# A gated linear attention with a two-layer network: its first step written on its own, and the order of the next three steps

## The chip, the cores and the metric

The kernel runs on one core of a Trainium2 chip. The metric is device time in microseconds (us) of one execution. Engines are named as the profile names them: PE multiplies matrices (PEld is its weight load), DVE and ACT work element by element, POOL is a third such engine and also issues DMAs, SP only issues DMAs.

## What is computed

```python
f = 1.0 / (1.0 + np.exp(-f_logit))                # B=4, H=8, S=768, D=48
for t in range(S):
    state = f[:, :, t, :, None] * state + np.einsum('bhd,bhe->bhde', k[:, :, t], v[:, :, t])
    y[:, :, t] = np.einsum('bhd,bhde->bhe', q[:, :, t], state)
x = y.transpose(0, 2, 1, 3).reshape(3072, 384)
h = x @ w_in                                      # 384 -> 2048
out = (np.maximum(h, 0.0) + alpha * np.minimum(h, 0.0)) @ w_out
```

## The kernel before, in words

The sequence is cut into 6 chunks of 128 times and the 4 batches into 2 pairs. A **step** is one chunk of one pair, so there are 12 steps, numbered by time: steps 0 and 1 are the first chunk of the two pairs (c is 0), steps 2 and 3 the second, and so on. Each step runs four generators, and an order written by hand as strings (FIRST for steps 0 to 3, USUAL for the rest) says which one is advanced next, up to its next `yield`. PE, DVE and ACT execute strictly in that order. SP and POOL are left to the framework's scheduler.

The letters of the order are these; a digit repeats the letter.

- `P` advances prepare (L258) of this step and `Q` that of the next step. It has six parts: (1) loads of f, q, k, v, a sigmoid and the products of q with up to three decays (qd, L287); (2) prefix and suffix scans (L317, L319); (3) scaled keys k4 and the first terms of us; (4) and (5) the other terms, kh, ks and q3; (6) the copies of q3 into A (L419).
- `O` advances carry, in two parts: first the products off (L444, L454), their copies into ad and A (L458, L462), the transposed keys pk (L471) and their copies ksn (L474); then the state products pd (L484) and moved(0), which puts them into vs (L500 for c = 0).
- `S` advances attend (six parts): for each of the two batches the score products raw (L520) and qu (L535) with masked copies into ad (L526, L541, L557); two parts of copies of ad into A (L563); the output products py (L574); and last moved(1), the copies of py to y (L583) and the ten DMAs that lay y out as xT (L603). In step 0 alone xT comes from twelve PE instructions with a constant `dense` (L592) and three ACT copies.
- `n` advances network of the **previous** step: eight parts with a product ph (L618) of 24 or 12 PE instructions, an ACT copy neg (L623) and two DVE gates (L625) each, then the second product. Of step 0 (`plain`) this is four parts of po (L638), the last of which ends with two ACT copies o (L644) and the stores: 12 parts. For the others it is seven half-size products (L657) with sums on DVE (L702): 13 parts.
- `a` and `b` load a piece of w_in and w_out (eight each) and convert it on ACT (L224, L225); `w` and `v` finish a piece on DVE (L234). ph number f of step 0 needs piece f of w_in. `W` (five parts, the first without work) forms differences of w_out on DVE (L721), which the networks after step 0 read.

PSUM has eight banks: two two-bank tiles (`psa`) for the attention products and four one-bank tiles (`psn`) for the network. At the start 52 small matmuls (L736) run on PE before any input is there. The buffers of f, q, k are single, so the next step's loads wait for the readers of this one.

In the order before, five of the six parts of prepare of step 1 stand in step 0 (`Q`), five of step 2 in step 1, and five of step 3 in step 2.

Of the kernel before, what the change touches and what calls it, by code (L numbers as in the profile page):

```python
# [17 lines left out]
C = 128  # L18
# [8 lines left out]
IDLE = 52  # L27
# [11 lines left out]
def flat(first, usual, steps=12):  # L39
    out = []  # L40
    left = {}
    for n in range(steps + 1):
        for key in (first[n] if n < len(first) else usual).split():
            for _ in range(int(key[1:] or 1)):
                k = key[0]
                if k in "awbvW":
# [12 lines left out]
def kernel(  # L59
# [60 lines left out]
    psn = ctx.enter_context(tc.tile_pool(name="psn", bufs=4, space=bass.MemoryType.PSUM))  # L120

    def pair(name):
        return psa.tile([128, 2, 512], F32, tag="pair", name=name)

    def bank(name):
        return psn.tile([128, 512], F32, tag="net", name=name)
# [35 lines left out]
    nc.gpsimd.memset(mquad, 0.0)  # L162
    for m in range(1, NB):
        lo = UO[m] + (4 if m == 1 else 0)
        n = NB - m
        nc.gpsimd.tensor_copy(mquad[:, lo:lo + 4 * n].rearrange("p (i r) -> p i r", r=4),
                              inq[:, 0:n].unsqueeze(2).broadcast_to((128, n, 4)))
    mhalf = const.tile([128, VW], F32, tag="mhalf", name="mhalf")
    nc.gpsimd.memset(mhalf, 0.0)
    for half in range(2):  # L170
        for m in range(1, NQ):
            n = NQ - m
            lo = 16 * half + 4 if m == 1 else VO[m] + 4 * n * half
            nc.gpsimd.tensor_copy(mhalf[:, lo:lo + 4 * n].rearrange("p (i r) -> p i r", r=4),
                                  inq[:, NQ * half:NQ * half + n].unsqueeze(2).broadcast_to((128, n, 4)))
# [7 lines left out]
    make_identity(nc, ident)  # L183
    nc.gpsimd.tensor_scalar(om, om, -1.0, 1.0, ALU.mult, ALU.add)


    dense = work.tile([128, DM], F32, tag="o", name="dense")
    nc.gpsimd.memset(dense, 0.0)
    for par in range(2):
        nc.gpsimd.tensor_copy(dense[:, (2 + par) * D:(3 + par) * D], ident[:, 64 * par:64 * par + D])  # L190
# [66 lines left out]

    def prepare(bp, c, x):  # L258

        i = f"{bp}_{c}"  # L260
        b0 = U * bp
        loads = nc.gpsimd if bp or c else nc.sync

        def load(name, src, bufs=2):
            t = work.tile([128, W], F32, tag=name, name=f"{name}_{i}", bufs=bufs)
            loads.dma_start(out=t.rearrange("p (u x) -> p u x", u=U),
                              in_=src[b0:b0 + U, c].rearrange("u p h t -> p u (h t)"))
            return t

        f = quads(load("f", fT, 1))  # L270
        q = load("q", qT, 1)
        k = x["k"] = load("k", kT, 1)

        for cc in range(NC2):
            t_, _ = halves(cc)
            loads.dma_start(out=vs[bp][t_, cc, :, 0:DM], in_=v[b0:b0 + U, c, t_].rearrange("u t d -> t u d"))


# [40 lines left out]
        nc.vector.tensor_tensor_scan(ss[:, ::-1], fs[:, ::-1], ones[:, ::-1], 0.0, ALU.mult, ALU.add)  # L319
        yield  # L320
# [57 lines left out]
        ended(0)  # L378
        if c:
            earlier(3)  # L380
        else:
            near(2, 1)
        ended(1)
        if c:
            earlier(4)
        else:
            nc.vector.tensor_tensor(k16[:, :, 0:16].rearrange("p g (i r) -> p g i r", r=4),
                                    k4.rearrange("p (g i r) -> p g i r", i=NB, r=4)[:, :, 0:NQ],
                                    g16[:, :, 0:NQ].unsqueeze(3).broadcast_to((128, G, NQ, 4)), ALU.mult)
        started(1)  # L390
        if c:
            earlier(5)
        else:
            near(3)
        yield
        if c:
            earlier(6)
        nc.vector.tensor_tensor(ks[:, :, 0], kh, f32[:, 1:G:2].broadcast_to((128, GC, DB)), ALU.mult)
        if c:
# [3 lines left out]
        else:  # L403
            nc.vector.tensor_tensor(q16.rearrange("p g (i r) -> p g i r", r=4), q4[:, :, NQ:NB], g16[:, :, NQ:NB].unsqueeze(3).broadcast_to((128, G, NQ, 4)), ALU.mult)
# [27 lines left out]
    def carry(bp, c, x):  # L432

        i = f"{bp}_{c}"
        q3, ks, kh, f64 = (x[n] for n in ("q3", "ks", "kh", "f64"))
        off = pair(f"off_{i}")
        for u in range(U):
            for hp in range(HP):
                for cc in range(NC2):
                    g = (u * HP + hp) * NC2 + cc  # L440
                    o = (u * HP + hp) * DB
                    for par in range(2):
                        r_ = rows(par)
                        nc.tensor.matmul(off[CH * cc:CH * cc + DB, par, o:o + DB],  # L444
                                         lhsT=kh[r_, g], rhs=q3[r_, g, 2], start=True, stop=True)
        if not c:
            for u in range(U):
                for hp in range(HP):
                    for j in range(NJ):
                        g = (u * HP + hp) * NJ + j  # L450
                        o = U * HP * DB + (u * HP + hp) * 16
                        for par in range(2):
                            r_ = rows(par)
                            nc.tensor.matmul(off[DB * j:DB * (j + 1), par, o:o + 16], lhsT=x["k16"][r_, g],  # L454
                                             rhs=x["q16"][r_, g], start=True, stop=True)
            for u in range(U):
                o = U * HP * DB + u * HP * 16
                nc.scalar.copy(ad[:, u, :, :, 16:DB], off[:, :, o:o + HP * 16].rearrange("p r (h t) -> p r h t", h=HP))  # L458
        for cc in range(NC2):
            s_ = slice(CH * cc, CH * cc + DB)  # L460
            for par in range(2):
                nc.scalar.copy(A[s_, :, par * HP:(par + 1) * HP, CH * cc + DB:CH * (cc + 1)],  # L462
                               off[s_, par, 0:U * HP * DB].rearrange("p (u h t) -> p u h t", u=U, h=HP))


# [333 lines left out]
```

## Time and profile before

| what | value |
|---|---|
| runs, median (range) | 622.3 us (620.87 to 622.85), 3 runs |
| profiled execution | span 622.1 us; the page gives no other time for it, and it lies within the runs |
| busy share of the span | PE 95%, PEld 85%, DVE 80%, ACT 40%, POOL 10% |
| first ph of the network of step 0 | starts 48.98 us |
| first ph of the networks of steps 1, 2 and 3 | start 102.47, 152.34 and 199.98 us |
| each step from then on | 47.7 us |
| DMA busy share, 0 to 40 us | 0.83 to 1.05 |

Times are counted from the start of the span. In a timeline row the first number is the start, the second the time from the first start to the last end of a merged group; brackets hold the idle time of the engine before it and what ended it. In a windows row each engine has its busy time and the number of instructions. A matmul of the program in fp32 shows as two records, each with a weight load of its own.

### The profile page before, as it was taken

How to read it: one execution, taken by the hardware profiler on the slowest of the kernel's cores; microseconds unless marked ns; L12 is line 12 of the kernel's file. 1: busy time of each engine (PE TensorE's matmuls, PEld its weight loads, DVE VectorE, ACT ScalarE, POOL GpSimd, SP SyncE). 2: the span in 40 equal slices, each digit the busy share in tenths (PEclk: the TensorE clock that was granted, in tenths of full speed). 3: DMA queues.
4: the chain of work that ended last, by engine and by line, in shares of the span. 5: the costliest groups of instructions: out<-in, count | busy, mean ns of one | idle time of the engine just before them, and what ended most of it. 6: DMA issues, size and time to landing. Idle time of an engine off the chain costs nothing.

```text
span 622.1 us, 19062 instructions
## 1 busy us (share of the span) xinstructions
PE 592.1 (95%) x8212; PEld 529.8 (85%) x8212; DVE 497.1 (80%) x997; ACT 246.6 (40%) x466; POOL 63.0 (10%) x117
## 2 busy tenths in 40 slices
PE   3568999999999999999999999999999999999997
PEld 3457866898899899899899899899889889889997
DVE  7588998899898798798798798798888888762261
ACT  5677862441641272262261351352253243223110
POOL 9120010001000011001001001001001000000000
PEclk9999999999999999999999999999999999999999
DMA  9964632014404314214313313413313401201000
GB/s 290 367 234 155 190 85 52 36 36 108 98 8 96 72 35 107 67 35 95 79 35 90 84 35 88 86 36 86 87 36 85 87 3 26 53 2 27 26 0 26
DMA packets 68116, 50.43 MB, mean 81 GB/s; under 512 B 47168, under 2 KB 60608, under 8 KB 68032
## 3 DMA queue, kind: packets, MB, share of 16 engines
q1 hardware_dynamic: 56656, 25.01, 15.6%
q0 software_dynamic: 6864, 22.35, 12.7%
q10 hardware_dynamic: 4512, 1.85, 1.7%
q8 instruction: 65, 1.06, 0.7%
q14 instruction: 19, 0.16, 0.1%
HBM read 36.21 MB, written 4.72 MB: 66 GB/s over the span
## 4 chain that ended last, share of the span: by engine, by line
PE 88%; DVE 6%; ACT 3%; issue 2%; DMA 1%; ACTq 0%; DVEq 0%
PE ph L618 39%; PE pc L657 9%; PE pa L657 8%; PE pd L657 5%; PE pe L657 4%; PE pb L657 4%; PE py L574 4%; PE po L638 3%; PE raw L520 3%; PE qu L535 3%; PE pd L484 3%; PE off L444 1%; PE xt L592 1%; DVE gate L625 1%; DMA f<-in_fT 1%
## 5 line engine op out<-in xcount | busy, mean ns | idle before, releaser
L618 PE MATMUL ph<-xT,w_in_sb 128*128 128x256 f32 x1152 | 258.7, 382 | 0.7 <-DVE Csum L661 0.7
L618 PEld LDWEIGHTS ph<-xT,w_in_sb 128*128 128x128 f32 x1152 | 216.4, 190 | 33.4 <-issue 2.3
L623 ACT ACTIVATE neg<-ph 128x512 f32<-128x512 f32 x96 | 57.4, 598 | 200.8 <-PE ph L618 139.5
L625 DVE SCALAR_TENSOR_TENSOR gate<-neg,om,ph 128x256 f32<-128x256 f32 x192 | 82.7, 478 | 50.6 <-ACT neg L623 50.4
L657 PE MATMUL pc<-t,S 128*128 128x192 f32 x352 | 61.7, 329 | 0.0
L657 PE MATMUL pa<-w_out_sb,gate 128*128 128x192 f32 x352 | 61.3, 327 | 0.1
L657 PEld LDWEIGHTS pa<-w_out_sb,gate 128*128 128x128 f32 x352 | 57.9, 190 | 1.0 <-DVE gate L625 0.4
L657 PEld LDWEIGHTS pc<-t,S 128*128 128x128 f32 x352 | 57.3, 190 | 0.6
L526 DVE COPY_PREDICATED ad<-mraw,raw 128x256 f32<-128x256 int32 (+1 forms) x96 | 42.4, 442 | 11.1 <-PE raw L520 8.6
L541 DVE COPY_PREDICATED ad<-mquad,qu 128x224 f32<-128x224 int32 (+6 forms) x140 | 42.0, 300 | 6.2
L419 ACT COPY A<-q 48x512 f32<-48x512 f32 x44 | 27.2, 619 | 36.1 <-DVE q L368 35.7
L563 ACT COPY A<-ad 32x256 f32<-32x256 f32 x96 | 38.7, 403 | 1.4
L330 DVE TENSOR_TENSOR us<-us,fs 128x768 f32<-128x768 f32 (+5 forms) x60 | 36.8, 614 | 0.0
L678 ACT ACTIVATE o<-pa 128x192 f32<-128x192 f32 x11 | 3.7, 332 | 75.2 <-PE pa L657 72.3
L661 DVE SCALAR_TENSOR_TENSOR Csum<-pc,Csum 128x192 f32<-128x192 f32 x22 | 7.9, 357 | 30.3 <-PE pc L657 30.1
L287 DVE TENSOR_TENSOR qd<-qd,f 128x768 f32<-128x768 f32 (+2 forms) x36 | 27.2, 756 | 6.0 <-ACT qd L282 6.0
L520 PEld LDWEIGHTS raw<-qd,k 48*32 48x32 f32 x1536 | 18.5, 109 | 15.3 <-issue 13.1
L520 PE MATMUL raw<-qd,k 48*32 48x80 f32 x1536 | 24.0, 243 | 7.6 <-issue 4.4
L702 DVE TENSOR_TENSOR S<-gate 128x512 f32<-128x512 f32 x44 | 30.3, 688 | 0.8
L657 PE MATMUL pe<-w_out_sb,S 128*128 128x192 f32 x176 | 30.4, 326 | 0.0
L657 PE MATMUL pd<-w_out_sb,S 128*128 128x192 f32 x176 | 30.4, 326 | 0.0
L657 PE MATMUL pb<-t,gate 128*128 128x192 f32 x176 | 30.4, 326 | 0.0
(101 smaller groups left out, 758.3 us busy)
## 6 DMA issues: line engine op xcount, KB each, us to landing
w_out_raw<-in_w_out SPq DMA_DIRECT2D x8, 767.8 KB, 5.8
w_in_raw<-in_w_in SPq DMA_DIRECT2D x8, 767.2 KB, 11.9
q<-in_qT POOLq DMA_DIRECT2D x11, 512.0 KB, 4.2
f<-in_fT POOLq DMA_DIRECT2D x11, 512.0 KB, 4.5
k<-in_kT POOLq DMA_DIRECT2D x11, 512.0 KB, 4.9
out<-o SPq DMA_DIRECT2D x24, 192.0 KB, 2.7
vs<-in_v POOLq DMA_DIRECT2D x22, 192.0 KB, 4.6
ksn<-kt SPq DMA_DIRECT2D x80, 32.0 KB, 2.0
```

Of the source, the lines that this page charges most:

```text
L287: nc.vector.tensor_tensor(qdv[d], qdv[d - 1][:, :, :, 1:5 - d], f[:, :, 1:5 - d].rearrange("p (g i) r -> p g i r", i=NB), ALU.mult)
L330: nc.vector.tensor_tensor(us[:, :, UO[m]:UO[m] + 4 * n].rearrange("p g (i r) -> p g i r", r=4), us[:, :, skip:skip + 4 * n].rearrange("p g ...
L419: nc.scalar.copy(A[halves(cc)[1], :, par * HP:(par + 1) * HP, CH * cc:CH * (cc + 1)], q3[rows(par)].rearrange("p (u h c) s t -> p u h c (s ...
L520: nc.tensor.matmul(raw[DB * j:DB * (j + 1), par, hp * C:hp * C + QW], lhsT=k[r_, g * DB:(g + 1) * DB], rhs=qd[r_, g], start=True, stop=True)
L526: nc.vector.copy_predicated(adu[:, :, :, d:4], mraw[:, d, :, d:4].bitcast(I32).unsqueeze(1).broadcast_to((128, H, NB, n)), rv[:, :, QO[d]: ...
L541: nc.vector.copy_predicated(ad[:, u, :, :, 4 * m:DB], mquad[:, lo:lo + n].bitcast(I32).unsqueeze(1).unsqueeze(1).broadcast_to((128, 2, HP, ...
L563: nc.scalar.copy(A[s_, u, :, s_], ad[s_, u].rearrange("p r h t -> p (r h) t"))
L618: nc.tensor.matmul(ph[:, j * T:(j + 1) * T], lhsT=w_in_sb[:, kt, m * 128:(m + 1) * 128], rhs=xT[:, kt], start=(kt == 0 and j == 0), stop=( ...
L623: nc.scalar.activation(neg, phv, AF.Relu, scale=-1.0)
L625: nc.vector.scalar_tensor_tensor(gate[:, m % NH, m // NH], neg[:, j], om[:, m:m + 1], phv[:, j], ALU.mult, ALU.add)
L657: nc.tensor.matmul(to[:, 0:DH], lhsT=of(f), rhs=by(f), start=(f == 0 and not more), stop=(f == NH - 1), skip_group_check=True)
L702: nc.vector.tensor_tensor(to, x_, y_, op)
```

## The change

Step 0 gets a generator of its own, `first_step` (letter `F`, eight parts). `C` emits the POOL constants and `L` the loads of step 1. The 52 early matmuls go. PSUM is split anew until step 0 ends: two two-bank tiles `psf` beside `psa`, closed when the first network bank is asked for.

In `first_step` the raw products of both batches follow at once on qd, those of qu (both batches in one tile) on the first terms of us; the two small products that `carry` put into `off` go to free columns of the raw tiles. The masked copies, the copies into A, py and xT are done batch by batch; six matmuls `warm` of the constant `ident`, whose results nothing reads, stand in between (4, then 2). moved(1) comes ahead of the xt products, which are now done for each batch, with six copies on ACT and DVE.

For c = 0, prepare is cut otherwise: part 2 holds one scan and all terms of us, part 3 k16 and q16, part 4 the suffix scan, kh and ks, part 5 the rest, and the copies of part 6 run on POOL. So do two of the eight copies of ad into A in step 0; two others run on DVE.

In the new order no part of step 1's prepare stands in step 0: its six `P` lie between the network parts of step 1. The last `S` of step 1 (moved(1), y, xT) and four `Q` of step 2 stand behind the twelfth `n`; the four `W` with work stand in step 2. From step 4 on the order is the same.

```diff
-IDLE = 52
...
 FIRST = (
-        "P5 a2 P a O w S w a w a2 S Q S O S w Q2 S Q2 S w",
-        "a2 w2 n O b w n b2 S P v2 n2 S b v Q n b n O S2 v n b v n Q2 b v Q b n S v2 W Q W S n2 W n",
-        "n S P n2 S W n W n O Q n3 O S Q n S Q n Q S2 Q n3",
-        "S n3 P S Q S n O n O n4 Q S Q S Q n S Q n Q n2",
+        "F C L F a2 F a F F F w F w F",
+        "w P a w n a w P n a w n a w n a w P n b P n b P n v O P n b v S n b2 v2 S O n v b2 S2 v n S v b v n S W Q4",
+        "n2 P n P S n W n S W n2 W n W O2 n Q n S2 Q n S Q n S Q n",
+        "P n P S n S n2 O2 n Q n3 Q n Q S3 n Q S n Q n Q n",
 )
...
-    psn = ctx.enter_context(tc.tile_pool(name="psn", bufs=4, space=bass.MemoryType.PSUM))
+    opening = ExitStack()
+    psf = opening.enter_context(tc.tile_pool(name="psf", bufs=2, space=bass.MemoryType.PSUM))
+    psn = []
...
-        return psn.tile([128, 512], F32, tag="net", name=name)
+        if not psn:
+            opening.close()
+            psn.append(ctx.enter_context(tc.tile_pool(name="psn", bufs=4, space=bass.MemoryType.PSUM)))
+        return psn[0].tile([128, 512], F32, tag="net", name=name)
...
+    def constants():
...
+    def fetch(bp, c, x):
+
+        if "fqk" not in x:
+            b0 = U * bp
+            loads = nc.gpsimd if bp or c else nc.sync
+
+            def load(name, src):
...
+            x["fqk"] = load("f", fT), load("q", qT), load("k", kT)
+            x["k"] = x["fqk"][2]
+            for cc in range(NC2):
+                t_, _ = halves(cc)
+                loads.dma_start(out=vs[bp][t_, cc, :, 0:DM], in_=v[b0:b0 + U, c, t_].rearrange("u t d -> t u d"))
+        return x["fqk"]
...
+        f, q, k = fetch(bp, c, x)
...
-        nc.vector.tensor_tensor_scan(ss[:, ::-1], fs[:, ::-1], ones[:, ::-1], 0.0, ALU.mult, ALU.add)
-        yield
+
+        def backward():
+            nc.vector.tensor_tensor_scan(ss[:, ::-1], fs[:, ::-1], ones[:, ::-1], 0.0, ALU.mult, ALU.add)
+
+        if c:
+            backward()
+            yield
...
+            near(2, 1)
+            near(3)
...
+            for to, of, ns in ((k16[:, :, 0:16], k4.rearrange("p (g i r) -> p g i r", i=NB, r=4)[:, :, 0:NQ], slice(0, NQ)),
+                               (q16, q4[:, :, NQ:NB], slice(NQ, NB))):
+                nc.vector.tensor_tensor(to.rearrange("p g (i r) -> p g i r", r=4), of,
+                                        g16[:, :, ns].unsqueeze(3).broadcast_to((128, G, NQ, 4)), ALU.mult)
+            yield
+            backward()
+            ended(0)
+            ended(1)
+            begun()
+            yield
+            started(1)
...
-                nc.scalar.copy(A[halves(cc)[1], :, par * HP:(par + 1) * HP, CH * cc:CH * (cc + 1)],
+                copy = nc.scalar.copy if c else nc.gpsimd.tensor_copy
...
+    def put(u, engines):
+        for j, engine in enumerate(engines):
...
+    def warm(n, to):
+        for _ in range(n):
+            nc.tensor.matmul(to[:, 0, U * HP * D:512], lhsT=ident, rhs=ident, start=True, stop=True)
+
+    def first_step(prep):
+
+        (bp, c), x = steps[0], run["x", 0]
+        i = f"{bp}_{c}"
+        next(prep)
+        raw = [pair(f"raw{u}_{i}") for u in range(U)]
+        for u in range(U):
+            raw_products(x, u, raw[u])
+        next(prep)
+        pk, qu = (pair(f"{n}_{i}", psf) for n in ("pk", "qu"))
+        for u in range(U):
+            quad_products(x, u, qu, C, VW, CH * u)
+        yield
+        next(prep)
+        edge, cross = (lambda hp: hp * C + QW + DB), (lambda hp: hp * C + QW)
+        for u in range(U):
+            half_products(x, u, raw[u], edge)
+        by_head = [r.rearrange("p r (h x) -> p (r h) x", h=HP) for r in raw]
+        for u in range(U):
+            nc.scalar.copy(ad[:, u, :, :, 16:DB].rearrange("p r h t -> p (r h) t"), by_head[u][:, :, edge(0):C])
+        yield
+        next(prep)
+        keys_products(x, pk)
+        keys_copies(x, i, pk)
+        yield
+        next(prep)
+        for u in range(U):
+            off_products(x, u, raw[u], cross)
+        pd = pair(f"pd_{i}", psf)
+        state_products(bp, x, pd)
+        warm(4, pd)
+        for u in range(U):
+            for cc in range(NC2):
+                s_ = slice(CH * cc, CH * cc + DB)
+                nc.scalar.copy(A[s_, u, :, CH * cc + DB:CH * (cc + 1)], by_head[u][s_, :, cross(0):edge(0)])
+        next(prep)
+        yield
+        moved(bp, c, x, pd, 0)
+        raw_copies(0, raw[0])
+        half_quad_copies(0, qu)
+        put(0, [nc.scalar, nc.gpsimd] * 2)
+        yield
+        raw_copies(1, raw[1])
+        half_quad_copies(1, qu, CH)
+        put(1, [nc.scalar, nc.vector] * 2)
+        py = pair(f"py_{i}")
+        y = work.tile([128, U, HP, C], F32, tag="ksn", name=f"y_{i}", bufs=1)
+        xT = x["T"] = work.tile([128, NK, T], F32, tag="xT", name=f"xT_{i}")
+        out_products(bp, 0, py)
+        warm(2, pd)
+        out_products(bp, 1, py)
+        yield
+        for u in range(U):
+            copy = (nc.scalar.copy, nc.vector.tensor_copy)[u]
+            copy(y[:, u].rearrange("p h t -> p (h t)"), py[:, u])
+        yield
+        moved(bp, c, x, pd, 1)
+        xt = [bank(f"xt{kt}_{i}") for kt in range(NK)]
+        for u in range(U):
+            for kt in range(NK):
+                pairs = [hp for hp in range(HP) if 2 * D * hp < 128 * (kt + 1) and 2 * D * (hp + 1) > 128 * kt]
+                for hp in pairs:
+                    o = 2 * D - 2 * D * hp + 128 * kt
+                    nc.tensor.matmul(xt[kt][:, u * C:(u + 1) * C], lhsT=dense[:, o:o + 128], rhs=y[:, u, hp],
+                                     start=(hp == pairs[0]), stop=(hp == pairs[-1]))
+                copy = nc.vector.tensor_copy if u and kt == 1 else nc.scalar.copy
+                copy(xT[:, kt, u * C:(u + 1) * C], xt[kt][:, u * C:(u + 1) * C])
         yield
...
-        for _ in range(IDLE):
-            nc.tensor.matmul(idle[0:32, 0:8], lhsT=ones[:, 0:32], rhs=ones[:, 0:8], start=True, stop=True)
+        pieces["F"] = first_step(run["P", 0])
...
+            if key[0] == "L":
+                fetch(*steps[key[1] + 1], run["x", key[1] + 1])
+            elif key[0] == "C":
+                constants()
+            else:
+                next(run[key] if key in run else pieces[key[0]])
```

More of the change, by code (lines that the diff above doesn't have):

```diff
@@ new lines, in keys_products, with keys_copies @@
+    def keys_products(x, to):
+        for u in range(U):
+            for hp in range(HP):
+                a = (u * HP + hp) * NC2
+                nc.tensor.transpose(to[:, u, hp * 128:(hp + 1) * 128],
+                                    x["ks"][:, a:a + 2].rearrange("p c s t -> p (c s t)"), ident)
+    def keys_copies(x, i, of):
+        ksn = x["ksn"] = work.tile([128, U, HP * 128], F32, tag="ksn", name=f"ksn_{i}", bufs=1)
+        for u in range(U):
+            nc.scalar.copy(ksn[:, u], of[:, u])
@@ new lines, in moved @@
+    def moved(bp, c, x, pd, cc):
+        of, to = halves(cc)[1], halves(1 - cc)[1]
+        was, then = (vs[bp][p, a, :, 0:DM].rearrange("p u (h e) -> p u h e", e=D)
+                     for p, a in ((of, cc), (to, 1 - cc)))
+        if c or cc:
+            nc.vector.tensor_tensor(then, was, x["f64"][of].unsqueeze(3).broadcast_to((D, U, H, D)), ALU.mult)
+        for par in range(2):
+            now = pd[rows(par), cc, 0:U * HP * D].rearrange("p (u h e) -> p u h e", u=U, e=D)
+            if c or cc:
+                nc.vector.tensor_tensor(then[:, :, par:H:2], then[:, :, par:H:2], now, ALU.add)
+            else:
+                nc.scalar.copy(then[:, :, par:H:2], now)
@@ L446, in carry @@
+    def carry(bp, c, x):
+        i = f"{bp}_{c}"
+        off = pair(f"off_{i}")
+        for u in range(U):
+            off_products(x, u, off, lambda hp: (u * HP + hp) * DB)
         if not c:
+            at = lambda u: U * HP * DB + u * HP * 16
             for u in range(U):
[L448 to L455, printed above, removed]
+                half_products(x, u, off, lambda hp: at(u) + hp * 16)
@@ L558, in attend @@
+            raw_products(x, u, raw)
+            raw_copies(u, raw)
+            qu = pair(f"qu{u}_{i}")
+            if c:
+                quad_products(x, u, qu, UW, UW)
+                quad_copies(u, qu)
+            else:
+                quad_products(x, u, qu, C, VW)
+                half_quad_copies(u, qu)
             yield
         for u in range(U):
[L561 to L563 removed]
+            put(u, [nc.scalar] * NJ)
```

292 lines of the change are left out of this document (130 added, 162 removed).

## The prediction, as it was written before the run

> **What bounds the kernel now.** I read the windows first, cut where the networks of steps 0, 1, 2 and 3 start (columns: length; busy time and instructions of PE, PEld, DVE, ACT, POOL; granted clock, DMA share, GB/s).
>
> ```profile
> 0.00:49.00 49.00, 26.11 (x701) 22.93 (x702) 37.00 (x66) 31.06 (x53) 19.87 (x49) 1.00 0.85 289
> 49.00:102.50 53.50, 51.63 (x746) 38.60 (x745) 47.82 (x85) 34.88 (x59) 4.46 (x7) 1.00 0.44 124
> 102.50:152.30 49.80, 48.99 (x785) 43.90 (x783) 44.70 (x88) 18.48 (x37) 4.47 (x7) 1.00 0.24 62
> 200.00:247.70 47.70, 47.63 (x657) 43.38 (x657) 40.83 (x85) 17.43 (x35) 4.47 (x7) 1.00 0.28 67
> ```
>
> From 49 us on PE is the bound, but DVE is close behind: 47.8 of 53.5 and 44.7 of 49.8 us. Before 49 PE is half idle, and DVE uses the time: 37 us of work, 13.1 of them prepare of step 1 (rows from 36.57 to 50.7, with a w of 1.0 between). The later steps take 47.7 us each whatever happens ahead, so the change is worth what it moves the start of step 3's network, 200.0 us now. Next the PE timeline of step 0:
>
> ```profile
> 24.51 1.06 PE L520 MATMUL raw<-qd,k 48*32 48x80 f32 x46 [1.76 <-ACT A L462]
> 26.67 0.56 PE L520 MATMUL raw<-qd,k 48*32 48x80 f32 x17 [1.10 <-issue]
> ...
> 29.48 1.04 PE L520 MATMUL raw<-qd,k 48*32 48x80 f32 x45 [1.40 <-DVE ad L526]
> 32.81 0.61 PE L520 MATMUL raw<-qd,k 48*32 48x80 f32 x18 [2.29 <-issue]
> ...
> 43.73 5.46 PE L592 MATMUL xt<-y,dense 128*128 128x256 f32 x12 [1.71 <-ACT y L583]
> 48.98 3.15 PE L618 MATMUL ph<-xT,w_in_sb 128*128 128x256 f32 x12
> ```
>
> Two stalls have no releaser but "issue". Between their ends lie 17+1+64+45 = 127 records and as many weight loads, and 6.14 us; the first comes after 104+64+128+8+46 = 350 records, that is 2 x 127 + 96. In the same places the DMA part shows a 16 KB packet of the instruction queue. So here PE gets some 127 records per 6.1 us, with two such blocks in hand at the start. [...]
>
> Last, the turn from network 0 to network 1 (step 1's py, y, xT; then o):
>
> ```profile
> 87.00 1.07 ACT L583 COPY y<-py 128x512 f32<-128x512 f32 x2 [0.28 <-PE py L574]
> ...
> 88.10 2.97 ACTq L603 DMA_DIRECT2D xT<-y  x4
> ...
> 102.02 0.49 ACT L644 ACTIVATE o<-po 128x384 f32<-128x384 f32 x1 [13.95 <-PE po L638]
> ```
>
> xT is ready some 10 us before network 1 needs it, because y stands ahead of the last po in ACT's queue.
>
> **Part 1, step 0: almost nothing won.** qd is ready at 10.63 as now. DVE drops one scan ahead of us (0.70, chain row L319) and reaches the end of near(3) at 15.1 (rows L321 to L344, 0.56 earlier, two more at 0.35). PE does raw from 10.7 to 13.6 (128 x 1.06/46) and qu from 15.15 (18 ns each). Without the 104 early records, I put the block borders at records 96, 223 and 350 again: raw passes 96 at 12.9, so the block after 223 is there at 19.0 and qu ends at 19.6; the half products (11 ns each) pass 350 at 20.7, wait for 25.1 and end at 25.4. Without fetch waits it would be 19.0 (DVE's q16 at 16.3, then qu to 17.5, then 1.43). Then ACT, in order: ad 0.45, two a 3.45 (pk 1.97 beside them), ksn 1.07, one a 1.75 (off and pd beside), A from raw 1.27: 33.4. raw tiles have two readers, ACT's A copies and DVE's masked copies; if the framework keeps two engines off one bank, DVE's 1.87 + 1.00 start only now, to 36.3; if not, they are long done and ACT's vs 0.96 and two put 0.82 end at 35.2. py(0) 1.85, warm 0.9, py(1) 1.85 (58 ns each, L574 here), y 0.6, w 1.0, moved(1) 2.07 on DVE follow: 43.5 or 45.6. xt takes banks of the closed pool in which pd lay, so it waits for moved(1); 24 records of half width at the xt row's pace (228 ns) are 5.5. Network 0 would start between 49.0 and 51.1. If fetch costs nothing it is 5 us earlier, if xt need not wait 3.7, if xt runs at ph's pace (5.38/24 = 224 ns a full record) 2.7: 37.6 at the earliest. Each wait is likelier than not, all three together hardly; I take **47**, call it T. The granted clock reads 1.00 throughout, so the rows show the two paces and not their cause. The dropped early matmuls lie in idle PE time and cost nothing by themselves.
>
> **Part 2, step 1: DVE's queue.** All of step 1's prepare now stands behind T. After xt's last copy DVE does a w 1.0 and part 1, which waits on ACT (sigmoid 1.06, kr 0.6, qd 1.0): it ends at T+6.35. Then in order to the first op of part 5: five w 5.0, six gate pairs 5.1, part 2 4.45, part 3 1.2, part 4 2.55, 0.6: T+25.3. Only then has PE off, half, pk (3.3) and ph 7 (2.7), ACT neg, DVE gate and v (2.4): po starts at T+34 (now 79.6-49 = 30.6 after ph, with raw, qu and pd of both batches done). PE then has 64 po at 0.327, the second batch 1.7, pd 0.95, py 2.1: 25.6. So po ends at **E = T+60** (now 53.3).
>
> **Part 3, the turn.** The last S stands behind the n whose o copies wait for the end of po. In ACT's queue: o 0.85, y 1.07, four xT issues 2.8, and only then step 2's sigmoid. xT begins to land at E+6.2 (3.1 to 3.9 from issue); PE idles so long, and nothing covers it. DVE, with only v's and moved(1) to do since T+35, starts step 2's prepare at E+6.
>
> **Part 4, step 2.** DVE's order up to the last gate of network 1: four Q 13.1 with ACT's qd (E+19.1), gates 1.7, part 5 4.1, six gate pairs 5.1, masked copies 2 x 4.17, sums 2.5, three W 5.5: E+46.3. All the products of L657 need that gate: 6 x 2.6, py 2.1, then y 1.07 and xT 4.2 with only pe (2.6) beside them: network 2 starts at **E+69.5** (now 50.0). Then a step of 47.7; what is left of DVE's lag I put into its 7 us of slack.
>
> **Sum.** 47 + 60 + 69.5 + 47.7 = 224.2 against 200.0 for the profiled execution of 622.1, which is at the median of the runs. That gives 24 us more: **646 us**. With T from 37.6 to 51.1 it is 637 to 650.
>
> POOL's copies are not in the sum. Three groups of rows bound them:
>
> ```profile
> 6.49 1.00 POOL L166 COPY mquad<-inq 128x28 f32<-128x28 f32 x7
> 7.44 3.24 POOL L174 COPY mhalf<-inq 128x12 f32<-128x12 f32 x6
> ...
> 12.16 2.19 POOL L190 COPY dense<-ident 128x48 f32<-128x48 f32 x2
> ```
>
> With DVE idle a copy takes 0.14, beside DVE's two-input products 0.54 and 1.1. [...]
>
> **Rivals.**
> - *Packed DVE (faster).* If the queues fit better than I read them, DVE's work alone decides: from T to network 2 it is 47.8 + 44.7 now, plus 13.1 of prepare and three w (3.0), less moved(1) of step 0 (2.1) and a fifth Q of step 3 (4.1): 102.4. With T at 42 network 2 starts at 144.4, not 152.3: **614**. For it: PE needs only 101. Against it: the o copies ahead of y, and 11 us in which DVE has nothing to do before E. It decides where DVE is idle for less than 8 us in that stretch.
> - *Only the turn costs (slower).* If PE carries step 2 in its 49 us after E+6.2: 47+60+6.2+49+47.7 = 210, **632**. For it: the work of DVE in step 2 today fits. Against it: 13 us of Q and 4 of part 5 stand ahead of the gates.
> - *POOL holds DVE up.* Six copies at 1.1 on top of the sum: **652**.
> - *It comes out even:* T 6 us earlier, the turn's 6 us lost, all else as now: **622**. Against it stands the same as against the packed case.
>
> **How the numbers follow.** The sum 0.63, only the turn 0.13, POOL 0.08, packed 0.13, even 0.03. About 0.3% is what a measurement of this kernel can tell from no change. Faster is 0.13, same 0.03, slower 0.84. The range leaves out the packed and even cases: 629 to 654.
>
> **What would show it.** Right: first ph between 44 and 51; "issue" stalls in the half products near 21; a PE gap of 5 us or more between po and ph L618 with o, y, xT in the chain; DVE idle over 10 us in the 25 before it; network 2 at 165 or later. Wrong: a T under 40, xT landing before po ends, or a first gate of network 1 ahead of step 2's scans.

## The result and the profile after

The changed kernel takes **658.0 us** (median of 4 runs, 657.3 to 658.9), the kernel before, on the same chip, 621.9 (620.9 to 622.9). The ratio is **1.0588, with a 95% interval of 1.0569 to 1.0608**: 36 us slower. The forecast was 646, range 629 to 654: the right sign, 12 us short. The profiled executions differ by 33.5 us (spans 655.6 and 622.1), 2.7 less than the medians, and the accounts below are of those. The profile of one experiment, e1_tail, was taken in a disturbed execution and is not read; its times are of undisturbed runs.

First the windows of the changed kernel, cut at the first ph of networks 0, 2 and 3 and around the turn from network 0 to network 1 (columns as in the prediction).

```profile
0.00:49.80 49.80, 21.86 (x621) 19.81 (x622) 28.09 (x51) 18.42 (x34) 19.16 (x51) 0.93 0.65 216
49.80:113.60 63.80, 54.55 (x746) 40.71 (x744) 41.19 (x73) 37.32 (x62) 4.60 (x7) 0.92 0.38 131
113.60:118.00 4.40, 0.08 (x2) 0.04 (x1) 0.00 (x0) 1.46 (x3) 1.08 (x2) 0.97 0.49 144
118.00:181.70 63.70, 51.83 (x657) 45.99 (x657) 59.80 (x110) 23.64 (x42) 5.92 (x9) 0.89 0.26 66
181.70:233.80 52.10, 51.42 (x785) 45.88 (x785) 45.87 (x97) 19.67 (x39) 4.47 (x7) 0.97 0.28 62
233.80:281.50 47.70, 47.59 (x659) 43.39 (x657) 41.50 (x87) 17.91 (x36) 4.47 (x7) 1.00 0.29 68
```

Network 0 starts at 49.8, where it started before (49.0), but VectorE has done 28.1 us of work by then, not 37.0. Network 1 starts 15.5 us late, network 2 29.3, network 3 33.8; from there on a step takes the 47.7 us that it took before. In 118 to 181.7 VectorE is busy 59.8 of 63.7 us and PE 51.8: VectorE is catching up.

TensorE's timeline of the first step shows what holds the start up.

```profile
15.46 1.43 PE L473 MATMUL qu<-us,k 48*32 48x52 f32 x94 [2.33 <-DVE us L356]
18.21 0.60 PE L473 MATMUL qu<-us,k 48*32 48x52 f32 x33 [1.32 <-issue]
...
24.78 0.50 PE L514 MATMUL raw<-us 48*32 48x16 f32 x34 [5.00 <-issue]
...
35.65 2.22 PE L567 MATMUL py<-A,vs 128*64 128x64 f32 x32 [2.32 <-POOL A L559]
...
44.83 5.13 PE L710 MATMUL xt<-y,dense 128*128 128x128 f32 x24 [4.62 <-DVE vs L551]
49.79 13.12 PE L725 MATMUL ph<-xT,w_in_sb 128*128 128x256 f32 x60
```

The two "issue" rows stand at records 222 and 350; the prediction had block borders at 223 and 350. xt waits for moved(1) (VectorE vs L551), as it had been read from the code.

The turn, on the timeline of all engines:

```profile
113.71 0.49 ACT L751 ACTIVATE o<-po 128x384 f32<-128x384 f32 x1 [0.15 <-PE po L745]
114.10 1.07 ACT L629 COPY y<-py 128x512 f32<-128x512 f32 x2
...
115.20 2.98 ACTq L637 DMA_DIRECT2D xT<-y  x4
...
117.99 2.47 PE L725 MATMUL ph<-xT,w_in_sb 128*128 128x256 f32 x5 [4.32 <-DMA xT<-y]
...
119.31 0.63 DVE L297 TENSOR_TENSOR kr<-f 128x256 f32<-128x256 f32 x1 [8.96 <-ACT f L286]
```

y stands behind the o copies in ScalarE's queue, the transposing loads behind y, and step 2's sigmoid behind those: PE idles 4.3 us and VectorE 9.0.

What VectorE waited for ahead of network 3 (waits: us in total, times, longest), first after, then before.

```profile
DVE ad L462 <- ACT A L681: 10.7, 1, 10.7
DVE kr L297 <- ACT f L286: 10.7, 3, 9.0
DVE gate L732 <- ACT neg L730: 10.0, 3, 7.9
DVE w_out_sb L238 <- ACT w_out_sb L229: 6.6, 3, 3.9
DVE xT L713 <- PE xt L710: 4.8, 1, 4.8
```

```profile
DVE gate L625 <- ACT neg L623: 10.5, 8, 2.5
DVE ad L526 <- PE raw L520: 8.1, 3, 6.2
DVE kr L290 <- ACT f L279: 1.2, 1, 1.2
```

### The profile page after: what moved, and what is told of

Its sections match the earlier page's. It is cut to its first block, busy times and chain, and to the rows that moved or that the text cites. A ratio compares the mean times of both kernels' runs of the same rounds, so it can differ in the third digit from the quotient of the medians.

```text
span 655.6 us, 18907 instructions
## 1 busy us (share of the span) xinstructions
PE 597.6 (91%) x8132; PEld 533.7 (81%) x8132; DVE 500.2 (76%) x1001; ACT 242.6 (37%) x459; POOL 64.9 (10%) x123
## 4 chain that ended last, share of the span: by engine, by line
PE 84%; DVE 9%; ACT 3%; issue 2%; DMA 1%; ACTq 1%; POOL 0%; DVEq 0%; POOLq 0%
PE ph L725 35%; PE pc L764 9%; PE pa L764 9%; PE pd L764 4%; PE pb L764 4%; PE py L567 4%; PE pe L764 4%; PE qu L473 3%; PE po L745 3%; PE pd L537 3%; PE raw L454 2%; PE off L505 1%; DVE gate L732 1%; DVE w_in_sb L238 1%; ACTq L637 1%
## 5 line engine op out<-in xcount | busy, mean ns | idle before, releaser
L725 PE MATMUL ph<-xT,w_in_sb 128*128 128x256 f32 x1152 | 264.3, 389 | 10.3 <-DMA xT<-y 4.3
L725 PEld LDWEIGHTS ph<-xT,w_in_sb 128*128 128x128 f32 x1152 | 220.7, 194 | 45.4 <-DMA xT<-y 4.9
L732 DVE SCALAR_TENSOR_TENSOR gate<-neg,om,ph 128x256 f32<-128x256 f32 x192 | 82.7, 478 | 49.7 <-ACT neg L730 48.8
L462 DVE COPY_PREDICATED ad<-mraw,raw 128x256 f32<-128x256 int32 (+1 forms) x96 | 42.3, 441 | 14.1 <-ACT A L681 10.7
L435 ACT COPY A<-q 48x512 f32<-48x512 f32 x40 | 24.7, 618 | 38.9 <-DVE q L382 38.5
L559 ACT COPY A<-ad 32x256 f32<-32x256 f32 x92 | 36.9, 401 | 4.2 <-DVE ad L497 2.8
L473 PE MATMUL qu<-us,k 48*32 48x112 f32 (+1 forms) x1536 | 27.4, 264 | 12.1 <-DVE us L342 8.0
L473 PEld LDWEIGHTS qu<-us,k 48*32 48x32 f32 x1536 | 22.3, 110 | 12.9 <-issue 12.3
L454 PEld LDWEIGHTS raw<-qd,k 48*32 48x32 f32 x1536 | 18.3, 109 | 17.6 <-ACT us L321 10.7
L454 PE MATMUL raw<-qd,k 48*32 48x80 f32 x1536 | 22.7, 243 | 10.7 <-DVE qd L294 10.7
```

Of the source, the lines that this page charges most:

```text
L454: nc.tensor.matmul(to[DB * j:DB * (j + 1), par, hp * C:hp * C + QW], lhsT=x["k"][r_, g * DB:(g + 1) * DB], rhs=qd[r_, g], start=True, stop ...
L462: nc.vector.copy_predicated(adu[:, :, :, d:4], mraw[:, d, :, d:4].bitcast(I32).unsqueeze(1).broadcast_to((128, H, NB, n)), rv[:, :, QO[d]: ...
L473: nc.tensor.matmul(to[DB * j:DB * (j + 1), par, o + 4:o + width], lhsT=x["k4"][r_, g * DB:(g + 1) * DB], rhs=x["us"][r_, g, 4:width], star ...
L559: copy(A[s_, u, :, s_], ad[s_, u].rearrange("p r h t -> p (r h) t"))
L725: nc.tensor.matmul(ph[:, j * T:(j + 1) * T], lhsT=w_in_sb[:, kt, m * 128:(m + 1) * 128], rhs=xT[:, kt], start=(kt == 0 and j == 0), stop=( ...
L732: nc.vector.scalar_tensor_tensor(gate[:, m % NH, m // NH], neg[:, j], om[:, m:m + 1], phv[:, j], ALU.mult, ALU.add)
```

## The experiments

All kernels were timed beside the kernel before (621.1 to 622.9 there). One table holds the measure that came to carry the explanation: VectorE's busy time up to network 3's first ph, and what is left to that point, its idle time.

| kernel | median us | ratio, 95% interval | first ph | network 3 | DVE busy to there | DVE idle |
|---|---|---|---|---|---|---|
| before | 621.9 | | 49.0 | 200.0 | 172.6 | 27.4 |
| after | 658.0 | 1.0569–1.0608 | 49.8 | 233.8 | 174.9 | 58.9 |
| e1_tail | 652.8 | 1.0460–1.0524 | | | | |
| e2_rows | 650.1 | 1.0434–1.0483 | 46.8 | 226.4 | 172.4 | 54.0 |
| e3_a_early | 658.1 | 1.0557–1.0617 | 50.8 | 234.1 | 174.8 | 59.3 |
| e4_raws3 | 663.2 | 1.0642–1.0700 | 48.2 | 237.0 | 174.8 | 62.3 |
| e5_xt_psa | 655.7 | 1.0525–1.0607 | 48.7 | 231.1 | 175.0 | 56.2 |
| e6_tail_xt | 650.6 | 1.0430–1.0479 | 48.8 | 227.4 | 175.0 | 52.4 |
| e7_best | 639.8 | 1.0260–1.0310 | 50.0 | 215.5 | 175.0 | 40.5 |
| e8_fill | 632.2 | 1.0153–1.0198 | 49.8 | 206.8 | 175.7 | 31.1 |
| e9_fill_xt | 627.4 | 1.0069–1.0121 | 49.9 | 204.0 | 175.8 | 28.2 |
| e10_rows23 | 657.3 | 1.0539–1.0603 | 50.4 | 233.6 | 175.6 | 58.0 |
| e11_tuned | 626.2 | 1.0041–1.0098 | 46.6 | 204.0 | 175.0 | 28.9 |
| e12_first_rows | 644.9 | 1.0349–1.0411 | 58.8 | 220.1 | 175.9 | 44.2 |

In every profile read here the span ends 421.7 to 422.3 us after network 3's first ph, so nothing behind that point matters.

**e1_tail: the last n of row 1 behind S and the quarters.**

```diff
-  "... S v b v n S W Q4",
+  "... S v b v S W Q4 n",
```

> The changed kernel with one edit in the order of step 1: its last S (moved(1), y, xT) and the four Q of step 2 stand ahead of the twelfth n, not behind it. Queue theory: ACT makes y while PE does the last po, so the 4.4 us gap of PE goes, and step 2's sigmoid starts near 112.3 in place of 118.2, so all of DVE's queue in step 2 is 6 us earlier: 652 us (651 to 653). Rival, PE carries step 2 and only the gap counts: 654 us. Rival, order of the tail does not matter: 658 us.

652.8: the queue of the turn is worth some 5 us. The rival's 654 lies just inside the interval (650.6 to 654.5), so this run alone hardly tells the two theories apart.

**e2_rows: the kernel before with the changed rows.** Its own first step; rows 1 to 3 are the changed ones, and row 0 is without the work that these put later.

```diff
-  "P5 a2 P a O w S w a w a2 S Q S O S w Q2 S Q2 S w",
+  "P5 a2 P a O S w S S O S w S2",
```

> The kernel before, its own first step kept, with the changed kernel's rows of the order for steps 1 to 3 and a row for step 0 that has the same letters left over (no Q, three a, two w). Queue theory: step 0 without other work reaches its first ph near 43 (41 to 46), and from there the rest is that of the changed kernel, 605.8 us from first ph to the end of the span, so 649 us of span and 651 us in all (648 to 654). Rival, the new first step is what costs: 622 to 626 us.

650.1: the order alone, with the old first step, costs 28 of the 36 us. That the time came as expected is in part luck: first ph was at 46.8 and not near 43, and from there to the end of the span it took 601.5 us and not 605.8. In its first 100 us VectorE is busy 64.7 us, in the changed kernel 65.1, before 82.4.

**e3_a_early and e4_raws3: the first step's stalls.** The third lift (a) ahead of the copies that wait for the half products; and three staging buffers for weight pieces in place of five.

```diff
-  "F C L F a2 F a F F F w F w F",
+  "F C L a3 F F F F F w F w F",
```

```diff
-RAWS, LEADS = 5, 4
+RAWS, LEADS = 3, 4
```

> The changed kernel with the three a of step 0 moved ahead of its second F, where ACT is idle (11.4 to 25.4 us). Chain theory: their 5.2 us of ACT lie between ad and A on the path to the first ph, so that starts near 45 (44.5 to 46) and the run takes 653 us. Rival, fetched instruction blocks or DVE are late next and give it back: first ph at 48 or later, 657 us.

> The changed kernel with three staging buffers of w_in and w_out in place of five, so that less weight traffic is in flight before 25 us. Fetch theory: the issue stall of 5.0 us in the half products is a block of instructions waiting behind that traffic; it shrinks to 1 to 3 us, the first ph comes at 46 to 48 and the run takes 655 us. Rival, the stall does not hang on the traffic: 5 us stay, 658 us.

Neither gave what was hoped. In e3 first ph came 1.0 later: the stage moved its stall to the next border of 127 records (record 477), on TensorE's timeline:

```profile
24.83 0.50 PE L514 MATMUL raw<-us 48*32 48x16 f32 x34 [4.74 <-issue]
...
32.26 1.06 PE L537 MATMUL pd<-vs,ksn 64*48 64x48 f32 x44 [3.16 <-issue]
```

In e4, with less in flight, the block came 5.75 us after the one ahead (qu's stalled row to the half products' row), not 6.57, and first ph 1.5 sooner. The run was 5 us slower all the same: in network 0 a later block border cost 2.52 us ahead of pd (0.34 in the changed kernel), and the 32 po behind it took 13.36 us in place of 10.59. VectorE waited longer for w_out (9.0 us, 6.6 in the changed kernel), but TensorE never waited for it. That load traffic lengthens a block is supported; it is a small part of the first step's stall.

**e5_xt_psa and e6_tail_xt: xt without the wait for moved(1); and e1's tail on top.**

```diff
-        moved(bp, c, x, pd, 1)
-        xt = [bank(f"xt{kt}_{i}") for kt in range(NK)]
+        both_ = pair(f"xt_{i}")
+        xt = [both_[:, kt // 2, (kt % 2) * T:(kt % 2 + 1) * T] for kt in range(NK)]
...
+        moved(bp, c, x, pd, 1)
```

> The changed kernel, with the PSUM tile of the xt products drawn from one of the psa pairs in place of the small pool that is given back, and moved(1) of the first step put behind xt and its copies. In the changed kernel xt waited 4.6 us for VectorE, that is for moved(1), and then took 5.1 us at 214 ns a product. Theory (the wait for moved(1) is paid whole by the first network): the first ph product starts some 6 us sooner, near 43.7 us, and the run takes about 652 us. Rival (VectorE or the next wait takes the time, since moved(1) has to be done ahead of step 1's first raw product all the same): first ph comes sooner, network 1 starts where it did, and the run takes 656 to 659 us.

> The kernel of the run before this one, with the tail of row 1 also as in the first experiment (n of network 1 behind the four fifths of the next step's quarters, not ahead of its S). Theory (first step and tail are separate stages of one chain): the two gains add, some 646 us, and step 2's ACT queue shows no 8 us wait of qu for VectorE's us. Rival (both take from the same VectorE backlog in step 2): 650 us or more.

The wait came back in two others: in one pair each group of xt waited for the copy ahead of it, and first ph waits for moved(1), 1.1 us sooner in all. e5 is a little faster than after, but its interval overlaps; it fits the rival better than the theory, though network 1 too came 2.4 us sooner. e6 shows e1's gain (5.1) with the turn's gap gone; the wait of qu for VectorE's us, which the theory wanted gone, is still 7.4 us.

**e7_best and e8_fill: the same first step, the gaps empty and filled.** e7 rewrites the first step (preparation, half, keys and off products first, moved(1) last, no warm products) and row 1, and takes rows 2 and 3 of before. e8 moves only work in the order, and its row 1 is that of before again; e8 against e7:

```diff
-  "F C L F Q2 F a F a F F w F F w",
-  "P n a w P n a w n P O P a w n S a w n ... v2 W S Q W n W",
+  "F C L a2 F Q2 F a F F Q w F a w F Q a2 w F Q w w",
+  "a2 w2 n O b w n b2 S P v2 n2 S b v Q n b n O S2 v n ... W",
```

> A first step written anew with PSUM banks of its own: all parts of the four networks' preparation and the half products ahead of xt, no warm loop, xt in a psa pair, moved(1) last; two of step 1's quarters and the planned a's beside network 0; row 1 with its state products behind the networks they belong to; rows 2 and 3 as in the kernel before. Theory (the change lost by its queues, not by having a first step of its own): first ph near 43 us, network 2 near 145 to 150 us, the run 615 to 620 us, below the kernel before. Rival (the blocks of instructions and VectorE's preparation of step 1 hold the first step again, whatever its order): network 2 at 155 us or later, the run 622 to 632 us.

> The first step of the run before this one (e7_best) unchanged, with only the order of the rest changed: the lifts of the first weight pieces by ScalarE (a, six in place of two ahead of network 0), their rounding sums on VectorE (w, five in place of two) and five quarters of step 1's preparation (in place of two) stand inside the first step, where VectorE and ScalarE sat idle, and rows 1 to 3 are word for word those of the kernel before. In e7_best VectorE had been busy 67.8 of the first 100 us, in the kernel before 82.4, in the changed kernel 65.1. Theory (what the new first step and its rows leave undone on VectorE and in the weights is what they lose): network 0 runs through without waits for w_in and w_out, VectorE's busy time in the first 100 us comes back to some 80 us, network 1 starts within 4 us of the kernel before, and the run takes 621 to 628 us though first ph is no sooner than 50. Rival (the half pace of TensorE and the blocks of instructions cost the time, whatever VectorE has done): VectorE's busy time comes back but the run stays at 634 to 640 us.

e7 missed its 615 to 620 by 20 us: its first ph was no sooner, and network 0 ran into weights that were not rounded yet. VectorE's and TensorE's timelines of e7:

```profile
69.44 1.06 DVE L238 TENSOR_TENSOR w_in_sb<-w_in_sb,w_in_lead 128x768 int16<-128x768 int16 x1 [5.13 <-ACT w_in_sb L229]
```

```profile
88.35 2.86 PE L722 MATMUL ph<-xT,w_in_sb 128*128 128x256 f32 x12 [2.37 <-DVE w_in_sb L238]
91.14 0.94 PE L537 MATMUL pd<-vs,ksn 64*48 64x48 f32 x64
95.31 10.59 PE L742 MATMUL po<-w_out_sb,gate 128*128 128x384 f32 x32 [3.23 <-DVE w_out_sb L238]
```

e8 starts network 0 at the same time (49.8) with the same stall of 5.0 ahead of it, and takes 632.2: 7.7 us less for moving lifts, rounding sums and quarters into the first step's gaps. Windows of e8 and of e7, the first 100 us:

```profile
0.00:100.00 100.00, 66.65 (x1323) 53.22 (x1324) 78.89 (x136) 61.61 (x105) 26.87 (x62) 0.93 0.63 205
```

```profile
0.00:100.00 100.00, 59.09 (x1239) 48.33 (x1240) 67.78 (x123) 52.52 (x92) 23.20 (x57) 0.97 0.58 192
```

The theory's direction holds and network 0's weight waits are gone; its size does not (632 where 621 to 628 was expected): network 1 starts 7 us after before's (109.5, 102.5), not within 4. ScalarE's work moved with VectorE's (busy 61.6 us in place of 52.5, VectorE 78.9 in place of 67.8), and VectorE itself had waited 5.1 us for ScalarE's lift in e7, so e8 doesn't tell which engine's work was the price.

**e9_fill_xt and e11_tuned: an earlier first ph on top.**

```diff
-        both_ = pair(f"xt_{i}")
-        xt = [both_[:, kt // 2, (kt % 2) * T:(kt % 2 + 1) * T] for kt in range(NK)]
+        both_ = [pair(f"xt0_{i}"), pair(f"xt1_{i}", psf)]
+        xt = [both_[kt % 2][:, kt // 2, 0:T] for kt in range(NK)]
```

and, from there to e11, with both y copies on ScalarE:

```diff
-  "F C L a2 F Q2 F a F F Q w F a w F Q a2 w F Q w w",
+  "F C L a2 F Q F a F F Q w F F F Q a3 w Q2 w3",
```

> The kernel of e8_fill with the xt products in two PSUM pairs in turn (one of psa, one of psf) in place of one, so that a group of products no longer waits for the copy of the group before it. In e7_best the six groups stood 1.58 us apart, of which the products took 1.22 and the wait 0.35. Theory (xt is on the chain of the first network, and the network on the chain of the end): first ph 2 to 3 us sooner than in e8_fill and the run 2 to 3 us shorter. Rival (VectorE sets when network 0 goes on, so that an earlier first ph only waits longer): first ph sooner by as much, the run within 1 us of e8_fill.

> The kernel of e9_fill_xt with less in the way of the first network's chain: one of step 1's quarters ahead of the masked copies in place of two (the second now behind them), both y copies on ScalarE, moved(1) straight behind the xt products, and the later lifts and rounding sums behind it. Theory (the chain of the first step sets the run now that VectorE's and the weights' work is in its gaps): first ph near 47 us in place of 49.9, the run 624 to 626, still not below the kernel before. Rival (VectorE ends its part no sooner, so that the gates of network 0 wait): 627 to 629.

e9 is 4.8 us faster than e8, but not for the reason given: first ph did not move (49.9). The 2.7 us by which the profiled spans differ arise in network 0, most of them at one block border (TensorE's timelines of e8 and of e9):

```profile
73.26 0.20 PE L473 MATMUL qu<-us,k 48*32 48x52 f32 x1 [2.97 <-issue]
73.39 7.13 PE L722 MATMUL ph<-xT,w_in_sb 128*128 128x256 f32 x24
```

```profile
72.34 5.45 PE L722 MATMUL ph<-xT,w_in_sb 128*128 128x256 f32 x24 [0.32 <-issue]
```

Why the border cost 2.97 in one and 0.32 in the other is open; the DMA share from 69 to 73.3 us was 0.59 in e8 and 0.15 in e9.

e11, in which some lifts and sums also stand later, has first ph 3.3 us sooner, network 3 at 204.0 as in e9, and a run 1.2 us shorter with intervals that overlap. In the time (626.2, at the edge of the 624 to 626 expected) it agrees with the theory. As the rival says, the lead was lost behind first ph: off waited 0.86 for VectorE's q, raw 2.37 for a copy on ScalarE, and a block border cost 2.52 where e9 lost 0.32; at 72.49 (e9: 72.34) the lead was gone. But that is not the wait of the gates for VectorE that the rival named. None of the versions beat the kernel before; the best is 0.4 to 1.0% slower.

**e10_rows23: rows 2 and 3 of before.**

```diff
-  "... S v b v n S W Q4",
-  "n2 P n P S n W n S W n2 W n W O2 n Q n S2 Q n S Q n S Q n",
-  "P n P S n S n2 O2 n Q n3 Q n Q S3 n Q S n Q n Q n",
+  "... S v b v n S W Q5",
+  "n W S P n2 S W n W2 n O Q n3 O S Q n S Q n Q S2 Q n3",
+  "S n3 P S Q S n O n O n4 Q S Q S Q n S Q n Q n2",
```

> The changed kernel with its rows 2 and 3 put back to those of the kernel before; rows 0 and 1 keep their order (the last four quarters of row 1 become five, since row 2 then holds one preparation less, and row 2 keeps four W). In the changed kernel the network of step 2 took 52.1 us from its first ph to that of the next step, in the kernel before 47.7. Theory (rows 2 and 3 as rewritten put a step's S behind the next network's first ph, so that its raw and qu products are paid in both): that network takes 48 to 49 us and the run is 3 to 5 us shorter, 653 to 655. Rival (VectorE's lag from step 1 sets this network, whatever its rows say): 657 to 659.

The step behind network 2's first ph now takes 47.5 us, but network 2 starts 4.4 us later, and network 3 starts where it did (TensorE's timeline of e10):

```profile
163.60 0.59 PE L764 MATMUL pa<-w_out_sb,gate 128*128 128x192 f32 x2 [1.29 <-DVE gate L732]
...
186.10 8.04 PE L725 MATMUL ph<-xT,w_in_sb 128*128 128x256 f32 x36 [0.61 <-DVE Csum L768]
...
233.58 5.45 PE L725 MATMUL ph<-xT,w_in_sb 128*128 128x256 f32 x24
```

The time is the rival's. The rows decide in which of the two steps the time is counted, and not the sum: from network 1's start to network 3's it is 114.7 us here and 115.8 in the changed kernel. VectorE is busy 63.4 of the 67.2 us ahead of network 2, so its lag fits as the cause, though nothing here shows it apart.

**e12_first_rows: the changed first step, untouched, with before's rows.**

```diff
-  "F C L F a2 F a F F F w F w F",
+  "F C L F a2 F Q F a F F w F w a F Q4 a2 w3",
```

> The changed kernel with its first step's functions untouched and only the order rewritten: rows 1 to 3 word for word those of the kernel before, and in row 0, beside the first step, what the kernel before has there: six lifts, five rounding sums and five quarters of step 1's preparation (one quarter ahead of the masked copies, four behind xt). Theory (what the run loses is VectorE's idle time ahead of network 3, 58.9 us in the changed kernel, 27.4 in the kernel before, and the order of the rows makes most of it): VectorE idles 32 to 37 us there, and the run takes 627 to 634 us. Rival (the new first step, as it stands, costs some 20 us by itself): 640 us or more.

644.9: by its time the rival's. VectorE's and TensorE's timelines say why:

```profile
30.75 0.63 DVE L297 TENSOR_TENSOR kr<-f 128x256 f32<-128x256 f32 x1 [11.59 <-ACT f L286]
```

```profile
36.25 1.08 PE L505 MATMUL raw<-q,kh 48*32 48x32 f32 x64 [9.05 <-DVE q L382]
```

The quarter's sigmoid stands in ScalarE's queue behind the ad copies, which wait for the stalled half products, so VectorE idles 11.6 us all the same; and the first step's own q now stands behind that quarter. This order did not fill the gap; in e7 and e8, where it is filled, all of the first step's preparation comes first. Other orders of this first step weren't tried. So this run tells what one placement costs, and not what the first step costs with a good one.

## Why the prediction was short

Its mechanism held: the work moved out of the idle first 49 us came back behind it, with VectorE busy nearly all the time in step 2. Its sum put network 3 at 224.2; it started at 233.8. Three terms were 11.0 us short and one 1.4 too long, which makes the 9.6. The other 2.4 us of the 12 are no event of the kernel: the sum took the span of 622.1 for the median time, and the changed kernel's span of 655.6 is 2.4 below its median.

Two steps failed. T was taken below the 49.0 to 51.1 that its own chain gave, and came 2.8 us later. And TensorE's own work behind the first step was priced too low, by 8.2 us: at full pace and without borders of blocks in step 1, and at the 47.7 us of the later steps in the step behind network 2. First what stood in step 1, on TensorE's timeline of the changed kernel, then the same products in the kernel before:

```profile
77.85 0.62 PE L514 MATMUL off<-us 48*32 48x16 f32 x38 [1.47 <-issue]
78.41 1.97 PE L521 MATMUL pk<-ident,ks 128*128 128x128 f32 x8
80.16 4.45 PE L725 MATMUL ph<-xT,w_in_sb 128*128 128x256 f32 x12
```

```profile
54.85 1.09 PE L471 MATMUL pk<-ident,ks 128*128 128x128 f32 x8
55.78 2.76 PE L618 MATMUL ph<-xT,w_in_sb 128*128 128x256 f32 x12
```

- **Part 1, T.** The chain had given 49.0 to 51.1 and 47 was taken, since "all three together hardly". All three were there: blocks of instructions (1.32 and 5.00), xt behind moved(1) (4.62), xt at the slow pace (214 ns a record of half width). So was a fourth, on which the 51.1 hung, the two readers of the raw tiles: the products into them ended at 28.2, and VectorE's masked copies began at 31.95, behind ScalarE's A L681. T was 49.8: **+2.8**, lost by not believing the chain. That nothing would be won here was right.
- **Part 2, step 1.** po ended at T+63.8, not T+60: **+3.8**. VectorE's q came late, as it said (off waited 3.93), but after it PE stalled three times more with no releaser but "issue" (1.47, 1.35 and 0.34; the first and the last at records 858 and 1239, whole blocks of 127 behind 350), and the next products ran at a slower pace: the 8 pk 0.9 us and the 12 ph 1.7 us longer than in the kernel before. Neither was in the sum; together they are more than the 3.8, and other parts went faster.
- **Part 3, the turn.** xT was there at E+4.4, not E+6.2, VectorE began step 2 at E+5.7 (E+6): right, and e1 gives it 5 us.
- **Part 4, step 2.** Network 2 started at E+68.1, not E+69.5: **−1.4**, right. The last gate of network 1 ended at E+45.8 (E+46.3). qu waited 8.0 for VectorE's us. The profile puts the 3.8 us pause ahead of network 2 down to VectorE too, but us is no input of ph. xT's loads were issued from 176.22 on and landed 2.2 to 5.2 us later, and in e3 the profile puts the same pause (3.88) down to them: it is the wait for xT that the sum had.
- **The step after.** 52.1, not 47.7: **+4.4**. "What is left of DVE's lag I put into its 7 us of slack": that slack was there, VectorE idled 6.2 us. TensorE was busy 51.4 of the 52.1. It did 785 records in place of 657, because the new rows put the raw and qu products of step 3's first batch behind network 2's first ph (1.8 us, from 186.12 to 187.89), and the sum had these 128 records nowhere; and the first 12 ph, behind the pause, took 1.7 us longer than at full pace. The remaining 0.9 are small waits and slower products.

The same step in the changed kernel (TensorE's timeline, with the pause and the 128 records) and its window in the kernel before:

```profile
181.68 4.51 PE L725 MATMUL ph<-xT,w_in_sb 128*128 128x256 f32 x12 [3.81 <-DVE us L342]
186.12 0.85 PE L454 MATMUL raw<-qd,k 48*32 48x80 f32 x60
...
186.83 1.13 PE L473 MATMUL qu<-us,k 48*32 48x112 f32 x62
187.89 2.86 PE L725 MATMUL ph<-xT,w_in_sb 128*128 128x256 f32 x12
```

```profile
152.30:199.98 47.68, 47.37 (x657) 42.93 (x657) 43.04 (x90) 20.41 (x39) 4.47 (x7) 1.00 0.31 70
```

*Packed DVE* (614) failed by its own condition: VectorE idled 13.1 of the 27.6 us ahead of the turn, and 9.0 across it. *Only the turn* (632) fell with e1, 5 us of 36. *POOL* (652) was near in time and wrong in cause: the profile shows no wait of VectorE for POOL ahead of network 3, and of POOL's copies only py's 2.3 us wait shows, and those copies began, like ScalarE's beside them, when VectorE's masked copies were done (35.21 and 35.14). *Even* is out. Of the signs named, first ph, the stalls near 21, VectorE's idle time and network 2's start came as written; the PE gap was 4.3 us, not 5.

What the runs put in place of the sum is shorter. VectorE's work up to network 3 is 172 to 176 us in every kernel here; the time is that work and VectorE's idle time ahead of it, 27.4 us before and 58.9 after. This is an identity: with the work fixed, idle time and the start of network 3 must move together, so the column shows where a kernel stands and not which wait costs it. What the experiments do show is that the displaced work is the cause in the main. Displacing it alone, with the old first step, costs 28 us (e2). Putting it back, with a first step rewritten so that its gaps can be filled, leaves 4 to 11 us (e8, e9, e11). Moving it into these gaps, with e7's first step unchanged, gains 7.7 (e8). An earlier first ph brought 1.2 of its 3.3 us, with intervals that overlap (e11). Not shown are the split between VectorE's sums and quarters and ScalarE's lifts, which moved together; and how much of the 36 us belongs to the first step's form is only bounded.

## What to carry to other kernels

When two engines are both near full, a kernel's idle opening is where the second one gets ahead: before taking its work out of there to start the first engine sooner, add up that engine's busy time to the point where the steady state begins, and count what becomes idle. A wait removed at the head of a chain is worth only what the waits behind it leave of it, so test a new order by when the steady state begins rather than by when the first product runs. When a step is priced from an older profile, count the products that the new order puts into it, and price those behind a pause at the pace that the trace shows there. And where a chain worked out row by row gives a number, take it.

## What the runs showed of the hardware

- **TensorE after a pause.** In the changed kernel the granted clock is 0.50 in the stretches behind the pauses of 4.62 and 7.99 us; windows of the changed kernel:

```profile
44.00:48.00 4.00, 3.17 (x15) 3.21 (x16) 0.67 (x2) 0.77 (x3) 0.00 (x0) 0.50 0.02 4
136.00:140.00 4.00, 3.61 (x69) 2.95 (x70) 3.85 (x13) 2.46 (x4) 0.00 (x0) 0.50 0.23 36
```

The 64 qu behind the 8.0 us pause took 1.75 us; at 287.50, where PE ran on without a pause, 64 qu took 1.07. What follows a shorter pause can't be told from its length: in e11 24 records of ph took 6.76 us soon after a pause of 2.37 us and 5.34 us behind one of 2.52, and in the changed kernel 5.45 us, at a clock of 1.00, behind one of 2.16. Nor does the clock column always go with the pace: in the kernel before it reads 1.00 from the start, though its xt took 5.46 us for 12 records and its ph, at 55.78, 2.76.
- **Blocks of instructions.** In the changed kernel the block of 127 products and their loads behind record 222 took 6.57 us to the next while the DMA engines were full (busy share 0.96 from 18.2 to 24.8 us), and 5.75 in e4 with three staging buffers. Stalls of 1.32 and 5.00 us stood on the chain of the first step. That these are fetched blocks is inferred: the stalls stand at records 222, 350, 858 and 1239, which are 128, 4 x 127 and 3 x 127 apart (that of 1.35 us, at record 1188, is not in this series); the changed kernel has 8132 records of products and as many weight loads, and its page counts 64 packets of 16 KB on the instruction queue, so 254 instructions to a packet; and the DMA view has one such packet between 15 and 16 us and the next between 22.0 and 22.5, each 2 to 3 us before the products went on (18.21 and 24.78).
- **Two readers of the same tiles.** VectorE's masked copies read the raw tiles that ScalarE's four copies (31.20, 1.48 for all four) read too. The last products into these tiles ended at 28.2, and the masked copies began at 31.95, when the first two of the four were done; so of their 10.7 us of waiting at most 3.8 hang on the second reader, and the rest on the products. Whether the program's order alone or the hardware too keeps the two apart wasn't tried.
